# Decode attention with a 16384-long cache: PV with V as the moving operand, and TensorE's order written by hand

## The chip, the core and the metric

The kernel runs on one NeuronCore of a Trainium2 chip. The metric is the device time of one execution in microseconds (us), as the median of the runs. A profile of one execution shows every instruction on TensorE (PE; PEld is its weight load), VectorE (DVE), ScalarE (ACT), GpSimd (POOL) and the queue of SyncE (SP), and the DMA transfers.

## What is computed

One token attends with 32 heads over a cache of 16384 keys and values of width 128. The result goes through an output projection and is mixed, by a scalar gate, with a small gated MLP of the same token. All inputs are bfloat16.

```python
q = (x @ wq).reshape(B, Sq, H, Dh)                # 1 token, H = 32, Dh = 128
scores = einsum('bhqd,bhkd->bhqk', q, k_cache) * Dh ** -0.5
p = softmax(scores)                               # over 16384 keys
o = einsum('bhqk,bhkd->bhqd', p, v_cache)
a = o.reshape(B, Sq, H * Dh) @ wo
g = sigmoid((x * gate_w).sum(-1))
out = g * a + (1 - g) * gmlp(x)                   # gmlp: gelu, layernorm, two projections
```

K and V of one head are 4 MB each, so the caches are 256 MB in all, and each byte is used once.

## The kernel before

**Tiles.** The keys of a head are laid out with 128 consecutive keys per partition: `k_t` and `v_t` are tiles of 128 partitions with 128 slots of 128 values (`(j d)`), 4 MB each. `load_k` (L76) has three buffers, `load_v` (L81) two. Both are issued on SP's queue and wait there, in order, until a buffer is free: K's after the last score matmul that reads it, V's after the last matmul of `attend` that reads it.

**Scores.** There is no transposed K. `qb` holds q on all 128 partitions. `scores_half(h, s)` (L212) works on 64 of the 128 slots: VectorE multiplies K by q in place (L219), TensorE adds up the 128 products in 16 matmuls with the identity as weights (L222, each moves 512 columns, 64 slots of 8 values, into one PSUM tile `s_ps`), and VectorE reduces the remaining 8 values (L224). After the second half ScalarE takes the exponential of the 128x128 scores (L228), which gives `p_t` in bfloat16 and the sums in `L_sb`. `s_ps` has two buffers, so each half has one.

**PV.** `attend(h)` (L232) makes 128 matmuls: each has one slot of V (128 keys by 128 values) as weights and one column of p as the moving operand, and all add into the column h of `o_ps`.

**The loop** (L242): the scores run two heads ahead of PV (`AHEAD`). At head h it loads K of h + 2 and V of h, makes the first half of the scores of h + 2, PV of h, and the second half. After head 1 it calls `gate()` and `mixer()`, which have matmuls on TensorE with small steps of VectorE and ScalarE between them (L144 to L204). V of the last head comes in three pieces. After the loop come the loads of wo, the sum of the softmax denominators (L265), PV of the last head, a rearrangement, and 128 matmuls with wo.

**The order of instructions.** Each engine runs its instructions in the order in the program. That order is not the one in the text: a planner at build time simulates the program with costs of its own and gives each engine the instruction that is ready and stands first in the text. In the kernel before it does this for all engines. Its result for TensorE, from head 2 on, is 29 of a head's 32 score matmuls, then the 128 of PV of two heads before, then the remaining 3. Its result for VectorE is, in one head, first product, second product, first reduction, second reduction; at the start (heads 0 to 2) products of the next head are mixed in. `gate()` comes ahead of all scores, and `mixer()` after those of head 2.

Of the kernel before, what the change touches and what calls it, by code (L numbers as in the profile page):

```python
# [12 lines left out]
FP32 = mybir.dt.float32  # L13
# [4 lines left out]
def kernel(  # L18
# [15 lines left out]
    nc = tc.nc  # L34
# [3 lines left out]
    Dh = 128  # L38
    H = HDh // Dh
# [4 lines left out]
    NJ = Sk // P  # L44
# [7 lines left out]
    const = ctx.enter_context(tc.tile_pool(name="const", bufs=1))  # L52
    kv = ctx.enter_context(tc.tile_pool(name="kv", bufs=2))
    sp = ctx.enter_context(tc.tile_pool(name="sp", bufs=2))
    ps_s = ctx.enter_context(tc.tile_pool(name="ps_s", bufs=2, space=bass.MemoryType.PSUM))
# [18 lines left out]
    vtile = {}  # L74

    def load_k(h):  # L76
        t = kv.tile([P, NJ * Dh], BF16, name="k_t", tag="k", bufs=3)
        nc.sync.dma_start(out=t[:], in_=k_src[h])
        ktile[h] = t

    def load_v(h, cuts=()):  # L81
        t = kv.tile([P, NJ * Dh], BF16, name="v_t", tag="v")
        edges = [0, *cuts, NJ]
        for a, b in zip(edges[:-1], edges[1:]):
            nc.sync.dma_start(out=t[:, a * Dh:b * Dh], in_=v_src[h][:, a * Dh:b * Dh])
        vtile[h] = t
# [3 lines left out]
    ident = const.tile([P, P], BF16, name="ident")  # L90
# [12 lines left out]
                      in_=B_w_in.rearrange("(p c) f -> p (c f)", c=DC))  # L103
    w_out = const.tile([P, FhC, D], BF16, name="w_out")
    nc.sync.dma_start(out=w_out[:].rearrange("p k n -> p (k n)"),
                      in_=B_w_out.rearrange("(p k) n -> p (k n)", k=FhC))
# [3 lines left out]
    for c in range(DC):  # L110
        nc.tensor.matmul(xb_ps[:, c * P:(c + 1) * P], lhsT=x_row[0:1, c::DC], rhs=ones_row[0:1, :],  # L111
                         start=True, stop=True)
# [17 lines left out]
    for i in range(4):  # L130
        nc.vector.tensor_copy(out=sel[:, i, :].rearrange("h (m i) -> h m i", i=4)[:, :, i],
                              in_=ident[0:H, 0:H])

    a_ps = ps_1.tile([P, 512], FP32, name="a_ps")
    o_ps = ps_1.tile([P, H], FP32, name="o_ps")
    g_sb = const.tile([P, 1], FP32, name="g_sb")
# [4 lines left out]
    def gate():  # L141
        gw_ps = ps_m.tile([P, DC + 2], FP32, name="gw_ps", tag="mm")
        for c in range(DC):
            nc.tensor.matmul(gw_ps[:, c:c + 1], lhsT=gw_row[0:1, c::DC], rhs=ones_row[0:1, 0:1],  # L144
                             start=True, stop=True)
        nc.tensor.matmul(gw_ps[:, DC:DC + 2], lhsT=ones_row[0:1, :], rhs=wb_row[0:1, :],  # L146
                         start=True, stop=True)
        gw_col = const.tile([P, DC], BF16, name="gw_col")
        nc.vector.tensor_copy(out=gw_col[:], in_=gw_ps[:, 0:DC])  # L149
        nc.vector.tensor_copy(out=wbf[:], in_=gw_ps[:, DC:DC + 2])  # L150
        g_ps = ps_m.tile([P, 1], FP32, name="g_ps", tag="mm")
        for c in range(DC):
            nc.tensor.matmul(g_ps[:, :], lhsT=xb[:, c, :], rhs=gw_col[:, c:c + 1],
                             start=(c == 0), stop=(c == DC - 1))
        nc.scalar.activation(out=g_sb[:], in_=g_ps[:, :], func=ACT.Sigmoid)
        nc.scalar.activation(out=gm_sb[:], in_=g_ps[:, :], func=ACT.Sigmoid, scale=-1.0)


    def mixer():
        z_ps = ps_m.tile([P, FC], FP32, name="z_ps", tag="mm")  # L160
        w_in5 = w_in[:].rearrange("p c (e m k) -> p c e m k", e=2, k=FhC)
        for fc in range(FC):
            for c in range(DC):
                nc.tensor.matmul(z_ps[:, fc:fc + 1], lhsT=w_in5[:, c, fc // FhC, :, fc % FhC],  # L164
                                 rhs=xb[:, c, 0:1], start=(c == 0), stop=(c == DC - 1))
        z = const.tile([P, FC], FP32, name="z")
        nc.vector.tensor_copy(out=z[:], in_=z_ps[:])
        t = const.tile([P, FC], FP32, name="t")
        nc.vector.tensor_mul(out=t[:], in0=z[:], in1=z[:])
        nc.vector.tensor_scalar(out=t[:], in0=t[:], scalar1=0.044715, scalar2=1.0,  # L170
                                op0=ALU.mult, op1=ALU.add)
        nc.vector.tensor_mul(out=t[:], in0=t[:], in1=z[:])
        nc.scalar.activation(out=t[:], in_=t[:], func=ACT.Sigmoid, scale=1.5957691216057308)
        nc.vector.tensor_mul(out=z[:], in0=z[:], in1=t[:])
        stats = const.tile([P, 2], FP32, name="stats")
        nc.vector.reduce_sum(out=stats[:, 0:1], in_=z[:, FhC:FC], axis=AX.X)
        sq = const.tile([P, FhC], FP32, name="sq")
        nc.vector.tensor_mul(out=sq[:], in0=z[:, FhC:FC], in1=z[:, FhC:FC])
        nc.vector.reduce_sum(out=stats[:, 1:2], in_=sq[:], axis=AX.X)
        tot_ps = ps_m.tile([P, 2], FP32, name="tot_ps", tag="mm")  # L180
        nc.tensor.matmul(tot_ps[:, :], lhsT=ones_f[:, :], rhs=stats[:, :], start=True, stop=True)
        mv = const.tile([P, 2], FP32, name="mv")
        nc.vector.tensor_scalar(out=mv[:], in0=tot_ps[:, :], scalar1=1.0 / Fh, scalar2=0.0,
                                op0=ALU.mult, op1=ALU.add)
        var = const.tile([P, 1], FP32, name="var")
        nc.vector.tensor_mul(out=var[:], in0=mv[:, 0:1], in1=mv[:, 0:1])
        nc.vector.tensor_sub(out=var[:], in0=mv[:, 1:2], in1=var[:])
        rstd = const.tile([P, 1], FP32, name="rstd")
        nc.scalar.activation(out=rstd[:], in_=var[:], func=ACT.Sqrt, bias=eps_t[:, 0:1], scale=1.0)
        nc.vector.reciprocal(out=rstd[:], in_=rstd[:])  # L190
        z2n = const.tile([P, FhC], FP32, name="z2n")
        nc.vector.tensor_scalar(out=z2n[:], in0=z[:, FhC:FC], scalar1=mv[:, 0:1],
                                scalar2=rstd[:, 0:1], op0=ALU.subtract, op1=ALU.mult)
        nc.vector.tensor_scalar(out=z2n[:], in0=z2n[:], scalar1=wbf[:, 0:1],
                                scalar2=wbf[:, 1:2], op0=ALU.mult, op1=ALU.add)
        uf = const.tile([P, FhC], FP32, name="uf")
        nc.vector.tensor_mul(out=uf[:], in0=z[:, 0:FhC], in1=z2n[:])
        u = const.tile([P, FhC], BF16, name="u")
        nc.vector.tensor_scalar(out=u[:], in0=uf[:], scalar1=gm_sb[:, 0:1], scalar2=0.0,  # L199
                                op0=ALU.mult, op1=ALU.add)  # L200
        w_out4 = w_out[:].rearrange("p k (c m) -> p k c m", c=DC)
        for k in range(FhC):
            for c in range(DC):
                nc.tensor.matmul(a_ps[:, c:c + 1], lhsT=w_out4[:, k, c, :], rhs=u[:, k:k + 1],  # L204
                                 start=(k == 0 and c == 0), stop=False, skip_group_check=True)

    L_sb = const.tile([P, H], FP32, name="L_sb")
    p_sb = {}
# [3 lines left out]
    def scores_half(h, s):  # L212
        k3 = ktile[h][:].rearrange("p (j d) -> p j d", d=Dh)
        qh = qb[:, h * Dh:(h + 1) * Dh].unsqueeze(1).broadcast_to([P, NH, Dh])
        if s == 0:
            s_tile[h] = sp.tile([P, NJ], FP32, name="s_sb")
        s_sb = s_tile[h]
        ks = k3[:, s * NH:(s + 1) * NH, :]
        nc.vector.tensor_tensor(out=ks, in0=ks, in1=qh, op=ALU.mult)  # L219
        s_ps = ps_s.tile([P, NH, W], FP32, name="s_ps")  # L220
        for i in range(NS):
            nc.tensor.matmul(s_ps[:, :, :], lhsT=ident[:, :], rhs=ks[:, :, i * W:(i + 1) * W],  # L222
                             start=(i == 0), stop=(i == NS - 1))
        nc.vector.tensor_reduce(out=s_sb[:, s * NH:(s + 1) * NH], in_=s_ps[:, :, :],  # L224
                                axis=AX.X, op=ALU.add)
        if s == 1:
            p_t = sp.tile([P, NJ], BF16, name="p_t", bufs=4)
            nc.scalar.activation(out=p_t[:], in_=s_sb[:], func=ACT.Exp, scale=inv_sqrt_dh,  # L228
                                 accum_out=L_sb[:, h:h + 1])
            p_sb[h] = p_t  # L230

    def attend(h):  # L232
        v3 = vtile[h][:].rearrange("p (j d) -> p j d", d=Dh)
        for j in range(NJ):
            nc.tensor.matmul(o_ps[:, h:h + 1], lhsT=v3[:, j, :], rhs=p_sb[h][:, j:j + 1],  # L235
                             start=(j == 0), stop=(j == NJ - 1))

    AHEAD = 2
    for h in range(AHEAD):
        scores_half(h, 0)  # L240
        scores_half(h, 1)
    for h in range(H - 1):  # L242
        if h > 0:
            if h + AHEAD < H:
                load_k(h + AHEAD)
            load_v(h)
        if h + AHEAD < H:
            scores_half(h + AHEAD, 0)
        attend(h)
        if h + AHEAD < H:  # L250
            scores_half(h + AHEAD, 1)
        if h == 1:
            gate()
            mixer()
    load_v(H - 1, cuts=(64, 96))


    wo_t = kv.tile([P, H * D], BF16, name="wo_t", tag="k", bufs=3)
# [65 lines left out]
```

The softmax here doesn't subtract the row's maximum and nothing guards it: scores larger than these inputs give would overflow.

## Time and profile before

| | |
|---|---|
| median of 3 runs | 665.37 us (665.19 to 666.33) |
| the profiled execution | 665.35 us, span 663.6 us |
| TensorE busy | 429.9 us (65%) |
| VectorE busy | 331.0 us (50%) |
| ScalarE busy | 25.5 us (4%) |
| moved by DMA | 280.31 MB, mean 422 GB/s |
| mean granted TensorE clock | 0.701 |
| score matmuls, L222 | 1024, 310.5 us busy |
| products, L219 | 64, 280.5 us busy, 4421 ns each |
| PV, L235 | 4096, 108.7 us busy |
| reductions, L224 | 64, 44.2 us busy, 691 ns each |

"Busy" is the time in which an engine had at least one instruction under way. Matmuls are pipelined: one score matmul has a record of 376 ns or more, but they can start closer together than that. The granted clock is that of TensorE as a share of full speed. An idle time is put down to what ended it, so a wait for K on VectorE is one in which the landing of K was the last thing missing. Lines of the timeline give start, duration, engine, source line, operation, tiles, count, and in brackets the idle time before and what ended it.

### The profile page before, as it was taken

The page shows a single profiled execution, that of the slowest core. Times are in us where ns is not written, and L with a number is a line of the kernel's source. Part 1 is how long each engine was busy: PE and PEld are TensorE (multiplying, and loading weights), DVE is VectorE, ACT ScalarE, POOL GpSimd, SP SyncE. Part 2 cuts the span into 40 slices and gives each one's busy share as a digit, 9 for nine tenths or more (in the row PEclk, how much of TensorE's full clock was granted, in tenths as well). Part 3 has the DMA queues.
Part 4 walks back from the last instruction along what each step waited for, and adds up shares of the span by engine and source line. Part 5 has one row for each costly group of instructions (what it writes and reads, how often), then busy time and mean ns, then how long its engine had stood idle before and what let it go on. Part 6 is the DMA issues. An engine that isn't in the chain of part 4 may idle for free.

```text
span 663.6 us, 11270 instructions
## 1 busy us (share of the span) xinstructions
PE 429.9 (65%) x5387; PEld 234.3 (35%) x5387; DVE 331.0 (50%) x163; ACT 25.5 (4%) x81; POOL 0.7 (0%) x6
## 2 busy tenths in 40 slices
PE   2777666578566578755668766566766666776574
PEld 0335233344223334422334432333432333433253
DVE  1593655444565444555444556444556553456600
ACT  0402000000000000000000000000000000000000
POOL 0000000000000000000000000000000000000000
PEclk9897656877656677765677765678765667776665
DMA  9999999999999999999999999999999999999986
GB/s 379 439 424 434 426 432 430 432 429 429 432 434 428 431 428 434 433 427 428 434 424 436 430 426 436 430 426 435 427 432 436 424 433 430 428 435 429 428 326 275
DMA packets 10574, 280.31 MB, mean 422 GB/s; under 512 B 1182, under 2 KB 1184, under 8 KB 1568
## 3 DMA queue, kind: packets, MB, share of 16 engines
q1 hardware_dynamic: 10520, 279.58, 98.3%
q8 instruction: 42, 0.69, 0.4%
q14 instruction: 4, 0.03, 0.0%
q10 hardware_dynamic: 8, 0.00, 0.0%
HBM read 279.58 MB, written 0.00 MB: 421 GB/s over the span
## 4 chain that ended last, share of the span: by engine, by line
DMA 69%; PE 21%; DVE 9%; issue 0%; SPq 0%; ACT 0%; ACTq 0%; DVEq 0%
DMA k_t<-in_A_k_cache_dram 66%; PE s_ps L222 16%; DVE k_t L219 9%; PE o_ps L235 5%; DMA wo_t<-in_A_wo_dram 3%; DVE s_sb L224 0%; PE a_ps L285 0%; PE ltot_ps L265 0%; SPq L261 0%; SPq L69 0%; DVE rl L267 0%; ACT p_t L228 0%; PE rT_ps L290 0%; DVE resT L292 0%; DVE res L288 0%
## 5 line engine op out<-in xcount | busy, mean ns | idle before, releaser
L222 PE MATMUL s_ps<-k_t,ident 128*128 128x512 bf16 x1024 | 310.5, 470 | 202.7 <-DVE k_t L219 202.7
L219 DVE TENSOR_TENSOR k_t<-k_t,qb 128x8192 bf16<-128x8192 bf16 x64 | 280.5, 4421 | 43.6 <-DMA k_t<-in_A_k_cache_dram 43.6
L222 PEld LDWEIGHTS <-ident 128*128 128x128 bf16 x1024 | 114.6, 114 | 382.9 <-issue 229.2
L224 DVE TENSOR_REDUCE s_sb<-s_ps 128x64 f32<-128x512 f32 x64 | 44.2, 691 | 240.6 <-PE s_ps L222 240.6
L235 PEld LDWEIGHTS <-v_t 128*128 128x128 bf16 x4096 | 108.6, 97 | 12.7 <-DMA v_t<-in_A_v_cache_dram 5.5
L235 PE MATMUL o_ps<-p_t,v_t 128*128 128x1 bf16 x4096 | 108.7, 163 | 5.2 <-DMA v_t<-in_A_v_cache_dram 5.1
L228 ACT ACTIVATE p_t<-s_sb 128x128 bf16<-128x128 f32 x32 | 9.9, 309 | 593.2 <-DVE s_sb L224 593.2
L121 PE MATMUL q_ps<-wq_t,xb 128*128 128x512 bf16 x32 | 8.8, 445 | 10.7 <-DMA wq_t<-in_A_wq_dram 10.7
L121 PEld LDWEIGHTS <-xb 128*128 128x128 bf16 x32 | 3.6, 112 | 15.7 <-issue 12.2
L285 PE MATMUL a_ps<-o_5855,wo_t 128*128 128x1 bf16 x128 | 3.9, 165 | 4.2 <-DMA wo_t<-in_A_wo_dram 4.2
L124 DVE CAST qb<-q_ps 128x512 bf16<-128x512 f32 x1 | 0.7, 692 | 11.5 <-PE q_ps L121 11.5
L272 DVE TENSOR_TENSOR o_sb<-o_ps,rl 128x32 bf16<-128x32 f32 x1 | 0.2, 192 | 12.0 <-PE o_ps L235 12.0
L228 ACT ACTIVATION_READ_ACCUMULATOR p_t<-s_sb 128x1 f32 x32 | 6.0, 187 | 0.0
L285 PEld LDWEIGHTS <-wo_t 128*128 128x128 bf16 x128 | 3.6, 104 | 4.5 <-DMA wo_t<-in_A_wo_dram 4.5
L126 ACT CAST qb<-q_ps 128x512 bf16<-128x512 f32 x7 | 4.1, 586 | 15.3 <-PE q_ps L121 15.3
L288 DVE CAST res<-a_ps 128x4 bf16<-128x4 f32 x1 | 0.2, 162 | 7.9 <-PE a_ps L285 7.9
L149 DVE CAST gw_col<-gw_ps 128x4 bf16<-128x4 f32 x1 | 0.2, 162 | 6.5 <-PE gw_ps L146 6.5
L164 PEld LDWEIGHTS <-w_in 128*128 128x128 bf16 x56 | 3.2, 153 | 0.5 <-issue 0.5
L164 PE MATMUL z_ps<-xb,w_in 128*128 128x1 bf16 x56 | 3.1, 192 | 0.0
L228 ACT ACT_TABLE_LOAD x2 | 2.6, 1283 | 0.0
L204 PE MATMUL a_ps<-u,w_out 128*128 128x1 bf16 x28 | 0.9, 165 | 2.3 <-DVE u L199 2.3
L111 PE MATMUL xb_ps<-ones_row,x_row 1*128 1x128 bf16 x4 | 0.6, 305 | 2.0 <-DMA x_row<-in_A_x_dram 2.0
(60 smaller groups left out, 19.1 us busy)
## 6 DMA issues: line engine op xcount, KB each, us to landing
k_t<-in_A_k_cache_dram SPq DMA_DIRECT2D x32, 4096.0 KB, 41.8
v_t<-in_A_v_cache_dram SPq DMA_DIRECT2D x31, 4096.0 KB, 33.7
wq_t<-in_A_wq_dram SPq DMA_DIRECT2D x1, 4096.0 KB, 12.5
v_t<-in_A_v_cache_dram SPq DMA_DIRECT2D x1, 2048.0 KB, 9.8
v_t<-in_A_v_cache_dram SPq DMA_DIRECT2D x2, 1024.0 KB, 11.9
wo_t<-in_A_wo_dram SPq DMA_DIRECT2D x1, 2048.0 KB, 17.3
w_in<-in_B_w_in_dram SPq DMA_DIRECT2D x1, 1792.0 KB, 44.1
wo_t<-in_A_wo_dram SPq DMA_DIRECT2D x1, 1024.0 KB
```

Source lines behind the costliest of these rows:

```text
L111: nc.tensor.matmul(xb_ps[:, c * P:(c + 1) * P], lhsT=x_row[0:1, c::DC], rhs=ones_row[0:1, :], start=True, stop=True)
L121: nc.tensor.matmul(q_ps[:, :], lhsT=xb[:, c, :], rhs=wq[:, c, nb * QB:(nb + 1) * QB], start=(c == 0), stop=(c == DC - 1))
L124: nc.vector.tensor_copy(out=qb[:, 0:QB], in_=q_ps[:, :])
L126: nc.scalar.copy(out=qb[:, nb * QB:(nb + 1) * QB], in_=q_ps[:, :])
L164: nc.tensor.matmul(z_ps[:, fc:fc + 1], lhsT=w_in5[:, c, fc // FhC, :, fc % FhC], rhs=xb[:, c, 0:1], start=(c == 0), stop=(c == DC - 1))
L204: nc.tensor.matmul(a_ps[:, c:c + 1], lhsT=w_out4[:, k, c, :], rhs=u[:, k:k + 1], start=(k == 0 and c == 0), stop=False, skip_group_check=True)
L219: nc.vector.tensor_tensor(out=ks, in0=ks, in1=qh, op=ALU.mult)
L222: nc.tensor.matmul(s_ps[:, :, :], lhsT=ident[:, :], rhs=ks[:, :, i * W:(i + 1) * W], start=(i == 0), stop=(i == NS - 1))
L224: nc.vector.tensor_reduce(out=s_sb[:, s * NH:(s + 1) * NH], in_=s_ps[:, :, :], axis=AX.X, op=ALU.add)
L228: nc.scalar.activation(out=p_t[:], in_=s_sb[:], func=ACT.Exp, scale=inv_sqrt_dh, accum_out=L_sb[:, h:h + 1])
L235: nc.tensor.matmul(o_ps[:, h:h + 1], lhsT=v3[:, j, :], rhs=p_sb[h][:, j:j + 1], start=(j == 0), stop=(j == NJ - 1))
L285: nc.tensor.matmul(a_ps[:, c:c + 1], lhsT=wo4[:, k, c, :], rhs=o2[:, k:k + 1], start=False, stop=(k == H - 1), skip_group_check=True)
```

## The change

For the heads 0 to 28, `attend_wide` replaces `attend`. It exchanges the operands: four columns of p are the weights (128 keys by 4), and four slots of V, 512 columns, are moved. There are 32 such matmuls, and they add into a tile `d_ps` of 4 partitions by 512 columns. Of its 4x4 blocks of 128 columns only those on the diagonal hold a product of a p column with its own slot of V. ScalarE copies the tile to `d_sb` in SBUF, and `collect` adds the four diagonal blocks into column h of `o_ps`: four float32 matmuls, with a 4x128 block as weights and one column of a 4x4 identity as the moving operand. The heads 29 to 31 keep `attend`. `d_ps` gets two buffers of its own in the pool of `s_ps`.

The loop, with the scores of heads 0 and 1 ahead of it, is put under `tc.manual_schedule` for TensorE: in this stretch TensorE's instructions keep the order of the text. The other engines are still ordered by the planner. `collect(h)` stands after the second half of the scores of h + 2, and `gate()` and `mixer()` stand after `collect(1)`.

```diff
+    ident_f = const.tile([4, 4], FP32, name="ident_f")
+    nc.vector.tensor_copy(out=ident_f[:], in_=ident[0:4, 0:4])
...
+    R = 512 // Dh
+    diag = {}
+
+    def attend_wide(h):
+        d_ps = ps_s.tile([R, R * Dh], FP32, name="d_ps")
+        NG = NJ // R
+        for g in range(NG):
+            nc.tensor.matmul(d_ps[:, :], lhsT=p_sb[h][:, g * R:(g + 1) * R],
+                             rhs=vtile[h][:, g * R * Dh:(g + 1) * R * Dh],
+                             start=(g == 0), stop=(g == NG - 1))
+        d_sb = sp.tile([R, R * Dh], FP32, name="d_sb")
+        nc.scalar.copy(out=d_sb[:], in_=d_ps[:, :])
+        diag[h] = d_sb
+
+    def collect(h):
+        for r in range(R):
+            nc.tensor.matmul(o_ps[:, h:h + 1], lhsT=diag[h][:, r * Dh:(r + 1) * Dh],
+                             rhs=ident_f[:, r:r + 1], start=(r == 0), stop=(r == R - 1))
+
     AHEAD = 2
-    for h in range(AHEAD):
-        scores_half(h, 0)
-        scores_half(h, 1)
-    for h in range(H - 1):
-        if h > 0:
+    WIDE = H - 3
+    with tc.manual_schedule(engines={mybir.EngineType.PE}):
+        for h in range(AHEAD):
+            scores_half(h, 0)
+            scores_half(h, 1)
+        for h in range(H - 1):
+            if h > 0:
+                if h + AHEAD < H:
+                    load_k(h + AHEAD)
+                load_v(h)
             if h + AHEAD < H:
-                load_k(h + AHEAD)
-            load_v(h)
-        if h + AHEAD < H:
-            scores_half(h + AHEAD, 0)
-        attend(h)
-        if h + AHEAD < H:
-            scores_half(h + AHEAD, 1)
-        if h == 1:
-            gate()
-            mixer()
-    load_v(H - 1, cuts=(64, 96))
+                scores_half(h + AHEAD, 0)
+            if h < WIDE:
+                attend_wide(h)
+            else:
+                attend(h)
+            if h + AHEAD < H:
+                scores_half(h + AHEAD, 1)
+            if h < WIDE:
+                collect(h)
+            if h == 1:
+                gate()
+                mixer()
+        load_v(H - 1, cuts=(64, 96))
```

## The prediction

> **What bounds the kernel now.** I read the page's slices first, then the waits, then the timeline of one head. The slices:
>
> ```profile
> PE   2777666578566578755668766566766666776574
> PEclk9897656877656677765677765678765667776665
> DMA  9999999999999999999999999999999999999986
> ```
>
> The DMA row is full until the last two slices, and one head's K and V (2 x 4096 KB) take a nearly constant time: the first K product of head 3 starts at 69.34 us, that of head 31 at 619.64 us, 550.3/28 = 19.65 us a head. TensorE is busy, but at a clock that moves between half and full. The waits say how much room the compute has:
>
> ```profile
> DVE s_sb L224 <- PE s_ps L222: 240.6, 60, 7.0
> PE s_ps L222 <- DVE k_t L219: 202.7, 34, 7.9
> DVE k_t L219 <- DMA k_t<-in_A_k_cache_dram: 43.6, 30, 2.7
> SPq L78 <- PE s_ps L222: 28.6, 29, 4.2
> ```
>
> (columns: total us, times, longest). VectorE waits for K 30 times, 43.6/30 = 1.45 us each. That is all the room there is between K's arrival and the compute. VectorE and TensorE hand the work to each other in turn, as one head of the timeline shows:
>
> ```profile
> 324.91 8.76 DVE L219 TENSOR_TENSOR k_t<-k_t,qb 128x8192 bf16<-128x8192 bf16 x2 [1.36 <-DMA k_t<-in_A_k_cache_dram]
> 329.38 8.86 PE L222 MATMUL s_ps<-k_t,ident 128*128 128x512 bf16 x29 [6.56 <-DVE k_t L219]
> 335.55 0.69 DVE L224 TENSOR_REDUCE s_sb<-s_ps 128x64 f32<-128x512 f32 x1 [1.88 <-PE s_ps L222]
> 338.08 3.36 PE L235 MATMUL o_ps<-p_t,v_t 128*128 128x1 bf16 x128
> 341.30 1.44 PE L222 MATMUL s_ps<-k_t,ident 128*128 128x512 bf16 x3
> 342.78 0.69 DVE L224 TENSOR_REDUCE s_sb<-s_ps 128x64 f32<-128x512 f32 x1 [6.54 <-PE s_ps L222]
> 344.58 8.76 DVE L219 TENSOR_TENSOR k_t<-k_t,qb 128x8192 bf16<-128x8192 bf16 x2 [1.12 <-DMA k_t<-in_A_k_cache_dram]
> ```
>
> VectorE's order in a head is product, product, reduction, reduction, and the second reduction stands ahead of the next head's product. So a ring closes each head: product 4.43, semaphore 0.04, 29 score matmuls, 128 PV matmuls, 3 score matmuls, reduction 0.69, next product. Its length: over the 29 heads from head 3 on the 29 matmuls' records average 8.58 us, 8.42 from first start to PV's start; PV takes 3.22 to the next start; the three average 1.31. So 4.47 + 8.42 + 3.22 + 1.31 + 0.71 = 18.13 us, 1.52 under the 19.65 that DMA needs, which agrees with the 1.45 waited. The chain of waits puts 69% on DMA and shows this ring only at every third head.
>
> [...] each head's scores start 0.43 us apart, then 0.2155 (16 matmuls in 3.61 us, one record of 0.38: 3.23/15). PV's 3.22 us of one-column matmuls is already enough: of the 30 triples after it only 4 take 0.81 us, the others 1.10 to 1.44, with some at the slow pace. [...] the trace has 80 ns for 128x4 (L290) beside 97 for 128x128. [...]
>
> **The change part by part.**
>
> *Wide PV, heads 0 to 28.* Removed: 128 one-column matmuls, 3.22 us. Added: 32 matmuls of 4 weight columns with 512 moving columns. The trace has none with so few weight columns at this width; the nearest row is L222, the same 512 moving columns and full 128 rows, and V is read without a stride. I take its pitch: 32 x 0.2155 = 6.90 us warm, 32 x 0.43 = 13.8 cold. The weight load (80 to 97 ns) lies beside the matmul before it, as L222's does; so no gain or loss from it.
>
> *Hand order.* TensorE now does 16 scores, 32 wide PV, 16 scores, four collecting matmuls. All 64 wide ones lie inside the ring. Warm they take 64 x 0.2155 = 13.79 us. Cold start: the old 29 cost 8.42 - 29 x 0.2155 = 2.17 us over the warm pace, about ten slow matmuls. In the new ring TensorE streams nothing wide between its last score and the next head's first: reduction 0.71 + product 4.47 = 5.2 us, longer than the 3.22 of PV that pulls the clock down today. So I charge 2.17 once a head; between the halves and PV no gap is left, since V has landed (it waits only 8 times at L235 today) and the second product ends at 8.8 us, before the first 16 scores and PV are through. The three slow scores after PV (1.31) are gone, contained in the 64. Adding the last record's 0.16 drain:
>
> ring = 4.47 + 13.79 + 2.17 + 0.16 + 0.71 = 21.30 us, against 19.65 of DMA. It exceeds it by 1.65 a head. Rings from head 3's product to head 31's: 28, all with wide PV. 28 x 1.65 = +46.2 us. DMA can no longer lead: the stall at L219 on K goes away, and VectorE's wait for S takes its place.
>
> *Will the planner leave the reduction ahead of the next product?* The ring stands on this; only TensorE's order is fixed by hand, VectorE's is the planner's. It put PV after 29 scores everywhere, so in its clock V comes 13 matmuls after the second product made the second half possible: a transfer there lasts 2 products + 13 m, m its matmul. After V the new order has 48 m to the reduction, and the next K comes one transfer later. The reduction stays first if 48 m < 8.86 + 13 m, m < 0.253. With m = 0.2155 it does, by 1.3 us; with m = 0.43 it wouldn't. I take the first.
>
> *Copy of d_ps on ScalarE.* Bound: 0.59 (L126, 128x512) above; ScalarE is at 4%, and 16 scores (3.45 us) cover it. Without that cover: 0.6 a head.
>
> *Collecting matmuls.* Four float32 ones. L265 shows one as two records in 0.65 us: at most 2.6 us, at least 8 x 0.025 (PV's pitch) = 0.2. They stand after the last score, beside the 5.2 us in which VectorE has the ring: nothing. Without that cover up to 2.6 a head.
>
> *Gate and mixer held at h == 1.* Today they fill TensorE's holes: 22.07 to 22.97 and 59.83 to 68.52, 9.6 us with their VectorE steps, while K is awaited. By hand they stand after head 3's scores, and head 4's scores wait behind them. 9.6 - 5.2 = 4.4 if VectorE does its small steps first; 13 if they queue behind two products. I take 6, once.
>
> *Queues.* SP's loads are the same in number and order. V's buffer comes free when wide PV ends, K's after the second half. They wait longest in flight today (33.7 us for V, 41.8 for K, against some 9.8 of transfer each), so over 20 us of lead hides that.
>
> *Tail.* From head 31's product to the end 43.96 us today. If compute is late, V of head 30 is already there and the queue is empty: product 4.47, 16 scores 5.6, old PV 3.2, then V31 with 12.5 (wq's 4096 KB, issue to landing), wo 9.2, last steps 4.0: 39.0. Gain 4.9; 3 to 7 taken as bounds.
>
> Sum: 665.35 (the profiled execution: span 663.6 and 1.75 around it; the median of the runs is 665.37) + 46.2 + 6 - 4.9 = 712.7, so 713. Own range: cold start known to about 0.4 us a head (11), mixer 4.4 to 13, tail 3 to 7: 698 to 734.
>
> **The rivals.**
> (a) *The planner lets the next product go first.* Then VectorE takes K as it lands, the reduction follows, and TensorE alone counts: 13.79 + 2.17 + 2.6 = 18.6 us, under 19.65. DMA bounds as now, the mixer's delay is regained at about 1 us a head, and the old PV of head 29 comes 13 scores earlier, which lets V31 be issued up to 2.8 us sooner; DMA ran at 0.84 in that stretch (619.6 to 640), so up to 1.5 us may come back. 664.5 us, 663.5 to 667: not slower. For it: the product of head 1 does stand ahead of head 0's second reduction at the start (33.28 and 37.61 us), where K lay ready. Against: from head 3 on it never does. It decides as soon as the planner's matmul costs over 0.253.
> (b) *Four weight columns don't hold the clock.* [...] For: today's PV loses the clock. Against: it moves one column each, this moves 512.
> (c) *The clock survives the 5.2 us.* Ring 19.1, under DMA: 665 us. Against: the triples above.
>
> **How the numbers follow.** Forecast 0.64, (a) 0.26, (b) 0.06, (c) 0.04. About 0.2% (1.3 us) is what can be told from no change. Forecast and (b) are slower; (a) and (c) are mostly the same, 0.06 of their 0.30 faster, 0.02 slower: faster 0.06, same 0.22, slower 0.72. The range must reach (a): 663.5 to 735; only (b) and edges lie outside. The forecast alone: 698 to 734.
>
> **What would show it.** Right: 512-column PV at a 0.2155 pitch, head to head 21 us, no wait of L219 on K, DMA under 9 tenths and gaps in it, ten slow scores a head, the reduction ahead of the next product. Wrong: a reduction behind the next product (a), slow pitch within PV (b), fast first scores (c). A wait of the collecting matmuls on ScalarE would show that the copy's cover is gone.

## The result and the profile after

The changed kernel takes 701.36 us (median of 4 runs, 700.91 to 701.54) against 665.38 us: a ratio of 1.0537, with a 95% interval of 1.0519 to 1.0555. It is slower, as forecast, by 36 us where 47.6 were forecast. The profiled execution has a span of 699.7 us.

The slices of the changed kernel:

```profile
PE   2766749979877779777779777789777788777794
PEclk9999778999999888999888999888999988999975
DMA  9999999999999999999999999989999989998557
```

TensorE's clock is now near full speed almost everywhere (mean 0.883 in place of 0.701), and yet the kernel is slower: a faster clock is no aim in itself. The DMA row says little of the new bound: DMA is busy all the time from 150 to 350 us, as before, and 95% of it from 350 to 600 us, where it moves 396 GB/s in place of 430. It had a backlog to live on: K's loads took 41.8 us from issue to landing before and take 24.5 now. So the sign "DMA under 9 tenths" that the prediction named hardly came. The chain of work that ended last shows the change:

```profile
PE 67%; DVE 21%; DMA 11%; issue 0%; SPq 0%; ACT 0%; DVEq 0%
```

It was 69% DMA before. The waits:

```profile
DVE s_sb L227 <- PE s_ps L225: 323.9, 58, 10.7
PE s_ps L225 <- DVE k_t L222: 121.9, 30, 9.1
DVE k_t L222 <- DMA k_t<-in_A_k_cache_dram: 12.4, 3, 7.0
PE d_ps L250 <- DMA v_t<-in_A_v_cache_dram: 1.9, 1, 1.9
```

VectorE waits for K three times in place of 30, the last time at 127.8 us; after that the two engines wait for each other. One head of the timeline:

```profile
320.57 8.75 DVE L222 TENSOR_TENSOR k_t<-k_t,qb 128x8192 bf16<-128x8192 bf16 x2
325.03 4.92 PE L225 MATMUL s_ps<-k_t,ident 128*128 128x512 bf16 x16 [4.13 <-DVE k_t L222]
329.88 7.07 PE L250 MATMUL d_ps<-v_t,p_t 128*4 128x512 bf16 x32
336.89 3.63 PE L225 MATMUL s_ps<-k_t,ident 128*128 128x512 bf16 x16
340.44 1.05 PE L259 MATMUL o_ps<-ident_f,d_sb 4*128 4x1 f32 x8
340.55 0.69 DVE L227 TENSOR_REDUCE s_sb<-s_ps 128x64 f32<-128x512 f32 x1 [9.80 <-PE s_ps L225]
341.16 8.75 DVE L222 TENSOR_TENSOR k_t<-k_t,qb 128x8192 bf16<-128x8192 bf16 x2
```

Read it as a ring: product, 16 scores, 32 wide PV, 16 scores, second reduction, and the next head's product at once, without a wait for K. The collecting matmuls (1.05 us) lie beside the reduction and the product; the idle 4.13 us before the next scores is what is left of VectorE's turn. VectorE keeps this order also where the next K is there: that of head 17 landed at 342.78 us, and VectorE still sat idle for 9.80 us ahead of head 16's second reduction at 362.78 and began head 17's product at 363.39. From head 7 on (product at 152.40 us) to head 31 (658.60) every ring has this form: 506.2/24 = 21.09 us a head, where the kernel before took (619.64 - 147.23)/24 = 19.68.

### The profile page after: what moved, and what is told of

Its sections match the earlier page's. It is cut to its first block, busy times and chain, and to the rows that moved or that the text cites. A ratio compares the mean times of both kernels' runs of the same rounds, so it can differ in the third digit from the quotient of the medians.

```text
span 699.7 us, 6196 instructions
## 1 busy us (share of the span) xinstructions
PE 543.7 (78%) x2835; PEld 237.6 (34%) x2835; DVE 328.2 (47%) x164; ACT 39.5 (6%) x108; POOL 0.7 (0%) x6
## 4 chain that ended last, share of the span: by engine, by line
PE 67%; DVE 21%; DMA 11%; issue 0%; SPq 0%; ACT 0%; DVEq 0%
PE s_ps L225 38%; PE d_ps L250 28%; DVE k_t L222 18%; DMA k_t<-in_A_k_cache_dram 8%; DMA wo_t<-in_A_wo_dram 3%; DVE s_sb L227 2%; PE o_ps L239 0%; PE o_ps L259 0%; SPq L85 0%; PE a_ps L316 0%; SPq L292 0%; PE a_ps L207 0%; PE tot_ps L184 0%; SPq L69 0%; ACT rstd L192 0%
## 5 line engine op out<-in xcount | busy, mean ns | idle before, releaser
L225 PE MATMUL s_ps<-k_t,ident 128*128 128x512 bf16 x1024 | 285.2, 442 | 121.9 <-DVE k_t L222 121.9
L222 DVE TENSOR_TENSOR k_t<-k_t,qb 128x8192 bf16<-128x8192 bf16 x64 | 280.4, 4416 | 12.4 <-DMA k_t<-in_A_k_cache_dram 12.4
L250 PE MATMUL d_ps<-v_t,p_t 128*4 128x512 bf16 x928 | 205.0, 379 | 1.9 <-DMA v_t<-in_A_v_cache_dram 1.9
L225 PEld LDWEIGHTS <-ident 128*128 128x128 bf16 x1024 | 110.2, 110 | 282.8 <-issue 202.3
L250 PEld LDWEIGHTS <-p_t 128*4 128x4 bf16 x928 | 76.5, 85 | 128.0 <-issue 14.2
L254 ACT COPY d_sb<-d_ps 4x512 f32<-4x512 f32 x29 | 16.7, 575 | 464.1 <-PE d_ps L250 464.1
L259 PEld LDWEIGHTS o_ps<-ident_f,d_sb 4*128 4x128 f32 x232 | 27.9, 186 | 12.3 <-issue 12.3
L259 PE MATMUL o_ps<-ident_f,d_sb 4*128 4x1 f32 x232 | 30.4, 248 | 0.0
L239 PE MATMUL o_ps<-p_t,v_t 128*128 128x1 bf16 x384 | 10.3, 164 | 1.9 <-issue 1.9
L239 PEld LDWEIGHTS <-v_t 128*128 128x128 bf16 x384 | 10.2, 99 | 2.2 <-issue 1.9
## 6 DMA issues: line engine op xcount, KB each, us to landing
k_t<-in_A_k_cache_dram SPq DMA_DIRECT2D x32, 4096.0 KB, 24.5
```

The costliest lines, as they stand in the source:

```text
L250: nc.tensor.matmul(d_ps[:, :], lhsT=p_sb[h][:, g * R:(g + 1) * R], rhs=vtile[h][:, g * R * Dh:(g + 1) * R * Dh], start=(g == 0), stop=(g = ...
L254: nc.scalar.copy(out=d_sb[:], in_=d_ps[:, :])
L259: nc.tensor.matmul(o_ps[:, h:h + 1], lhsT=diag[h][:, r * Dh:(r + 1) * Dh], rhs=ident_f[:, r:r + 1], start=(r == 0), stop=(r == R - 1))
```

## The experiments

Nine kernels follow, each with its ratio to the kernel before, of runs on the same chip, and the 95% interval of that ratio. A head with the old PV is called narrow. Three theories stand against each other. *Ring*: the 64 wide matmuls of a head, a cold start among them (in the head above the first scores start 0.427 us apart, at a granted clock of 0.50 from 324.30 to 327.72 us, and the later ones 0.216 us apart, at 1.00), lie between a head's product and the next head's, because the second reduction stands ahead of that product on VectorE. *Occupancy*: TensorE simply has too much to do (78% busy). *Order by hand*, or later release of V's buffers, or contention: something beside the ring.

**1. Hand order, old PV everywhere.**

```diff
-    WIDE = H - 3
+    WIDE = 0
```

> Hand order on TensorE kept, PV of all heads the old way (128 one-column matmuls). Ring theory: product 4.4, 16 scores from a cold start 5.4, PV 3.2, 16 scores after PV, cold again for about 10 of them, 5.4, reduction 0.7 = 19.2 us a head, still under the 19.65 of DMA; DMA bounds, the mixer's place costs a few us that are hardly regained: 667 us (664 to 671). Rival, the hand order itself is what costs: 690 or more. Rival, TensorE's occupancy: 665.

Measured: 665.12 us, ratio 0.9998 (0.9989 to 1.0007). The hand order of TensorE costs nothing that can be told; the mixer's delay was regained too. The total came out as expected, its parts didn't: where K lay ready (heads 4 to 6) a narrow ring took 17.0 us in place of 19.2, since the 16 scores after PV ran at the full clock there (3.61 us).

**2. Wide PV, order left to the planner.**

```diff
-    with tc.manual_schedule(engines={mybir.EngineType.PE}):
+    if True:
```

> Wide PV kept, TensorE's order left to the planner (29 scores, 32 wide, 3 scores, mixer in the early hole; on VectorE the second reduction stands ahead of the next product in every head from 2 on). Ring theory: the same 64 matmuls in the ring, 21.1 us a head, in all 28 rings instead of 24, no delay by the mixer: 665 + 28 x 1.44 - 3 = 703 us (698 to 707). Rival, the hand order is to blame: 665 to 670.

Measured: 709.96 us, 1.067 (1.0654 to 1.0686). This is slower than with the hand order, and above the expected range (698 to 707). The 28 rings take (665.74 - 72.19)/28 = 21.20 us, 0.1 more than expected each (about 3 in all); head 3's product starts 2.9 us later (72.19 us in place of 69.30), and the tail is 1.5 longer than expected. So the loss came in with the exchange of operands and not with the order by hand, which even helped.

**3. The next head's product ahead of the second reduction.** VectorE's order by hand as well. `sums` is the matmul part of `scores_half`, `reduce` and `product` are its VectorE parts, i counts half heads, and the load of K moves up in the text with its product.

```diff
+        s_ps = sums(i)
+        if i + 2 < 2 * H and (i + 2) // 2 not in ktile:
+            load_k((i + 2) // 2)
+        reduce(i, s_ps)
+        if i + 2 < 2 * H:
+            product(i + 2)
...
-    with tc.manual_schedule(engines={mybir.EngineType.PE}):
+    with tc.manual_schedule(engines={mybir.EngineType.PE, mybir.EngineType.DVE}):
+        product(0)
+        product(1)
```

> The changed kernel with VectorE's order by hand as well: reduction of a half, product of the same half of the next head, so that the next head's product stands ahead of the second reduction and no head's product waits for the head before. All 64 wide matmuls, the copy and the collecting matmuls stay. Ring theory: TensorE needs 13.8 + 2 + 1 = 17 us a head, DMA 19.65 bounds again: 665 us (663 to 668). Rivals, TensorE's occupancy or the later release of the V buffers or contention on the memories: 695 to 702 as in the changed kernel.

Measured: 660.92 us, 0.9936 (0.992 to 0.9953). All of TensorE's work is still there, and 40 us are gone, 4 more than the change had cost, which puts it under the expected range (663 to 668); kernels 5 and 9 look for these 4 us. Its waits, and one head of its timeline:

```profile
DVE k_t L220 <- DMA k_t<-in_A_k_cache_dram: 247.7, 28, 15.7
PE s_ps L231 <- DVE k_t L220: 76.3, 29, 9.0
DVE s_sb L238 <- PE s_ps L231: 43.2, 26, 8.1
```

```profile
320.66 3.63 PE L231 MATMUL s_ps<-k_t,ident 128*128 128x512 bf16 x16
323.35 4.43 DVE L220 TENSOR_TENSOR k_t<-k_t,qb 128x8192 bf16<-128x8192 bf16 x1 [8.91 <-DMA k_t<-in_A_k_cache_dram]
324.22 1.05 PE L278 MATMUL o_ps<-ident_f,d_sb 4*128 4x1 f32 x8
327.69 0.68 DVE L238 TENSOR_REDUCE s_sb<-s_ps 128x64 f32<-128x512 f32 x1
327.83 5.30 PE L231 MATMUL s_ps<-k_t,ident 128*128 128x512 bf16 x16 [2.56 <-DVE k_t L220]
```

The product at 323.35 starts when K lands, while the scores of the head before still run; their reduction follows at 327.69. VectorE waits 8.9 us for K, TensorE is 81% busy. TensorE's work, the use of the buffers and the traffic are what they were, so occupancy, buffer release and contention fall. The edit also moves the load of K in the text; kernel 6 has it in the same place and is slow.

**4. More matmuls, to hold the clock.** After `collect(h)`:

```diff
+                f_ps = ps_m.tile([P, 512], FP32, name="f_ps", tag="mm")
+                for _ in range(11):
+                    nc.tensor.matmul(f_ps[:, :], lhsT=ident[:, :], rhs=qb[:, 0:512],
+                                     start=True, stop=True)
```

> The changed kernel plus 11 matmuls of 512 columns after the collecting ones of each head 0 to 28, into a scratch PSUM tile that nothing reads; VectorE's order as in the changed kernel from head 8 on. They lie in the 5.1 us in which VectorE has the ring. Ring theory with the cold start as the deciding term: the next scores start at the full clock, 16 take 3.5 us instead of 5.4, the ring falls from 21.1 to 19.1 us, under DMA's 19.65: 665 us (663 to 669), though TensorE does 11 x 29 = 319 more wide matmuls. If the clock doesn't matter: 701. If TensorE's occupancy bounds: 701 + 29 x 2.4 = 770.

Measured: 661.88 us, 0.9949 (0.9934 to 0.9964). One head:

```profile
330.36 0.69 DVE L227 TENSOR_REDUCE s_sb<-s_ps 128x64 f32<-128x512 f32 x1 [9.33 <-PE s_ps L225]
330.97 8.75 DVE L222 TENSOR_TENSOR k_t<-k_t,qb 128x8192 bf16<-128x8192 bf16 x2
331.24 2.55 PE L285 MATMUL f_ps<-qb,ident 128*128 128x512 bf16 x11
335.44 3.61 PE L225 MATMUL s_ps<-k_t,ident 128*128 128x512 bf16 x16 [1.66 <-DVE k_t L222]
350.25 8.75 DVE L222 TENSOR_TENSOR k_t<-k_t,qb 128x8192 bf16<-128x8192 bf16 x2
```

The order on VectorE is that of the changed kernel and the ring is closed, but its 16 first scores take 3.61 us in place of 4.9 to 6.5, and the granted clock is 1.00 from 200 to 640 us (0.89 in the changed kernel). The ring is 350.25 - 330.97 = 19.28 us, just under what K needs, and 319 additional matmuls make the kernel 40 us faster (a little under the expected 663 to 669). TensorE is 86% busy, the most of all. So two conditions had to meet for the loss: the ring and the cold start. Taking away either one ends it.

**5. The product first, with the old PV.** Kernel 3 with `WIDE = 0`.

> The kernel with the next head's product ahead of the second reduction, but with the old PV (128 one-column matmuls) in all heads. It asks where the 4 us under the kernel before come from. If from the order (V of head 31 asked for sooner, more room on VectorE): 661 us. If from the wide PV itself (half the instructions on TensorE, so less instruction fetch among the transfers, 0.36 in place of 0.69 MB): 664 to 665. I hold the second for more likely, since the hand order with the old PV gave 665.1.

Measured: 665.18 us, 0.9994 (0.9986 to 1.0003). Without the ring the wide PV is worth 4.3 us (3.9 by the two ratios, as kernels 3 and 5 ran on different chips), and the order alone nothing.

**6. The reduction first, in every head.** Kernel 3 with the product moved in front of its own scores from head 3 on:

```diff
         i = 2 * h + s
+        if h > AHEAD:
+            product(i)
         s_ps = sums(i)
...
-        if i + 2 < 2 * H:
+        if i + 2 < 2 * AHEAD + 2:
             product(i + 2)
```

> The changed kernel with VectorE's order by hand, but the dependent way round in every head from 3 on: product, reduction, product, reduction of one head, then the next head. The start (heads 0 to 2) is as before, the mixer's VectorE steps stand between head 3 and head 4. This is the case that the prediction priced: 28 rings and the mixer in the ring. Ring theory: 665.1 + 28 x 1.44 + 9 for the mixer - 3 in the tail = 712 us (708 to 717). If the order of the two on VectorE has no part in it: 661 as with the product first, or 701 as in the changed kernel.

Measured: 713.39 us, 1.0727 (1.071 to 1.0743). It comes out at the prediction's 713, in part by luck: its runs spread from 711.5 to 714.9, and two errors of the sum pull against each other. From head 4 to head 31 the rings are (670.02 - 98.84)/27 = 21.15 us, 1.50 over DMA's time in place of the 1.65 charged; head 3 to head 4 takes 98.84 - 69.20 = 29.6, so the mixer in the ring costs 8.5 in place of 6. Kernels 3 and 6 differ in nothing but the place of the product on VectorE, and 52 us lie between them.

**7. Wide PV in the second half only.** Kernel 6 with

```diff
-            if h < WIDE:
+            if 15 <= h < WIDE:
```

at both places.

> As the run with the reduction first in every head, but only the heads 15 to 28 have the wide PV, the heads 0 to 14 the old one. Ring theory: 14 wide rings at 21.1 us, the narrow ones at about 19.2 and so held by DMA at 19.5; the mixer's 9 us are partly regained before head 15: 665 + 14 x 1.44 + 4 - 3 = 686 us (682 to 692). If a wide head costs something that isn't a ring (contention, a one-time loss), the narrow heads would be slow as well or the sum would not be half.

Measured: 706.04 us, 1.0608 (1.0592 to 1.0625). The expectation missed by 20 us. A narrow head:

```profile
204.87 4.42 DVE L220 TENSOR_TENSOR k_t<-k_t,qb 128x8192 bf16<-128x8192 bf16 x1
209.34 5.10 PE L231 MATMUL s_ps<-k_t,ident 128*128 128x512 bf16 x16 [5.11 <-DVE k_t L220]
214.28 3.35 PE L260 MATMUL o_ps<-p_t,v_t 128*128 128x1 bf16 x128
214.55 0.69 DVE L238 TENSOR_REDUCE s_sb<-s_ps 128x64 f32<-128x512 f32 x1 [5.26 <-PE s_ps L231]
215.16 4.42 DVE L220 TENSOR_TENSOR k_t<-k_t,qb 128x8192 bf16<-128x8192 bf16 x1
219.63 5.08 PE L231 MATMUL s_ps<-k_t,ident 128*128 128x512 bf16 x16 [2.00 <-DVE k_t L220]
224.75 0.69 DVE L238 TENSOR_REDUCE s_sb<-s_ps 128x64 f32<-128x512 f32 x1 [5.17 <-PE s_ps L231]
225.36 4.42 DVE L220 TENSOR_TENSOR k_t<-k_t,qb 128x8192 bf16<-128x8192 bf16 x1
```

The second product now stands behind the first reduction. With the wide PV (7 us) that is covered; the old one (3.35 us) is too short to cover 0.7 + 4.4, so both products and both cold starts lie in the ring: 225.36 - 204.87 = 20.49 us, again over DMA. The edit had made a second ring. The same sum gives its length, but the run says nothing on the half.

**8. The same with the changed kernel's order:** both products of a head, then both reductions.

```diff
+    held = []
...
-        if h > AHEAD:
-            product(i)
+        if h > AHEAD and s == 0:
+            product(i)
+            product(i + 1)
...
+        if h <= AHEAD or s == 1:
+            if s == 1 and h > AHEAD:
+                reduce(i - 1, held.pop())
+            reduce(i, s_ps)
+        else:
+            held.append(s_ps)
```

> The half-wide kernel once more, with VectorE's order as the changed kernel has it in its late heads: both products of a head, then both reductions, then the next head. PV of the heads 15 to 28 is wide, of 0 to 14 old; the mixer's VectorE steps stand between head 3 and head 4. Ring theory: narrow rings 4.4 + 5.4 + 3.2 + 5.1 + 0.7 = 18.8 to 19.3 us, under DMA, so most of the mixer's 9 us is regained; then 14 wide rings at 21.1: 665 + 2 + 14 x 1.5 - 3 = 685 us (681 to 691). If the loss isn't the ring's, near 701 or near 665.

Measured: 681.78 us, 1.0253 (1.0239 to 1.0267), at the lower end of what was expected. Where the narrow part ends and the wide one begins:

```profile
325.07 8.76 DVE L221 TENSOR_TENSOR k_t<-k_t,qb 128x8192 bf16<-128x8192 bf16 x2 [2.33 <-DMA k_t<-in_A_k_cache_dram]
344.49 8.76 DVE L221 TENSOR_TENSOR k_t<-k_t,qb 128x8192 bf16<-128x8192 bf16 x2 [1.76 <-DMA k_t<-in_A_k_cache_dram]
366.49 8.75 DVE L221 TENSOR_TENSOR k_t<-k_t,qb 128x8192 bf16<-128x8192 bf16 x2
387.73 8.75 DVE L221 TENSOR_TENSOR k_t<-k_t,qb 128x8192 bf16<-128x8192 bf16 x2
```

The narrow part keeps DMA's pace: the product of head 17 starts at 344.49 us, as in the kernel before (344.58), and VectorE waits for K ahead of it. From there the heads are (640.87 - 344.49)/14 = 21.17 us apart and no wait for K is left. Each wide head adds to the loss, and the narrow heads had made up for the mixer.

**9. Where the 4 us come from.** Kernel 3 with small matmuls after `collect(h)`:

```diff
+                f_ps = ps_m.tile([P, 512], FP32, name="f_ps", tag="mm")
+                for _ in range(84):
+                    nc.tensor.matmul(f_ps[:, 0:1], lhsT=ident[:, :], rhs=qb[:, 0:1],
+                                     start=True, stop=True)
```

> The fastest kernel so far (next product ahead of the second reduction, wide PV, 660.9 us) plus 84 matmuls of one column after the collecting ones of each head 0 to 28, into a scratch tile that nothing reads. They take about 84 x 0.027 = 2.3 us a head on TensorE, whose 17 us then come to 19.3, still under DMA's 19.5, and bring the number of TensorE's instructions back to about that of the kernel before. If it is the fewer instructions, and with them fewer instruction fetches among the transfers (0.36 MB in place of 0.69), that make the wide PV 4 us faster where it isn't in a ring: 664 to 666 us. If it is the way in which V is read: 661.

Measured: 663.94 us, 0.998 (0.9973 to 0.9986): 3.0 of the 4.3 us are gone again. The row of the instruction fetches in the list of DMA queues (transfers, MB, share), of kernel 3 first and of this kernel second:

```profile
q8 instruction: 22, 0.36, 0.2%
```

```profile
q8 instruction: 41, 0.67, 0.4%
```

K arrives every (616.47 - 69.29)/28 = 19.54 us in kernel 3, every 19.65 in this one, in kernel 5 and in the kernel before: 3.1 us over the 28 heads. TensorE isn't what is waited for (VectorE waits for K for 235 us in all). So K came later with more TensorE instructions. The starts of the products show in which steps. From head 9 on most heads are 19.3 to 19.7 us apart in these four kernels, and the difference sits in single heads that take 20.6 to 21.0: heads 14, 20 and 27 in the kernel before and in kernel 5, 15, 21 and 28 here, but only 14 and 29 in kernel 3. From the product of one of these to that of the next the fetch queue made eight transfers, of 16 KB and about 1.07 us each, in all four kernels, though that took 293 us in kernel 3 and 118 or 138 in the others. So the delay goes with the fetches, about 1.4 us for eight of them; how a fetch holds up K is not shown. The last 1.3 us lie at the end: from the product of head 31 kernel 5 takes 43.8 us, this one 42.5 and kernel 3 42.4. What causes them stays open.

## Why the prediction was right, and where its sizes were off

The span grew by 699.7 - 663.6 = 36.1 us: 39.0 between the products of head 3 and head 31 (589.3 in place of 550.3), and -2.9 after that. The prediction had 46.2 + 6 - 4.9 = 47.3.

*The bound: 1.5 us of room a head.* Right. Kernel 8 shows it from both sides: with the old PV K is waited for, with the wide one it isn't.

*Wide PV, 6.90 us by L222's pitch.* Right: 7.00 us for 32. The loads of the four-column weights lie beside the matmuls, which start 0.216 us apart. Those loads are hardly shorter than full ones (records of 85 ns, against 97 in the old PV), so the few columns saved nothing. The granted clock is 1.00 through the wide PV of all 29 heads; rival (b), whose time was an estimate, is out. V was waited for once. (The 8 waits at L235 that the prediction counts are four, each seen by the matmul and by its load.)

*The cold start, 2.17 us a head.* Right in kind, a little large: over the 24 rings from head 7 on the first 16 scores average 5.35 us up to PV's start, 1.90 over 3.45. Kernel 4 shows that this term decides: without it the ring is under DMA's time. Rival (c), that the clock survives the gap, was wrong, but its arithmetic (19.1 us) is what kernel 4 measured once the gap was filled (19.28).

*The ring, 21.30 us.* Measured 21.09: the first scores are 0.27 less, the reduction 0.10 less, since the next product starts just before it ends, wide PV and the second half together 0.16 more.

*"28, all with wide PV", and "the reduction stays first".* This is the term that was mis-sized. From head 6 on the planner did keep the reduction first, as the sum in matmul costs had it. For two heads after the mixer, 4 and 5, it did not. Here the first product of head 5 stands ahead of the second reduction of head 4, and that of head 6 ahead of the one of head 5:

```profile
111.65 4.41 DVE L222 TENSOR_TENSOR k_t<-k_t,qb 128x8192 bf16<-128x8192 bf16 x1
121.60 0.69 DVE L227 TENSOR_REDUCE s_sb<-s_ps 128x64 f32<-128x512 f32 x1 [5.54 <-PE s_ps L225]
127.80 4.42 DVE L222 TENSOR_TENSOR k_t<-k_t,qb 128x8192 bf16<-128x8192 bf16 x1 [0.58 <-DMA k_t<-in_A_k_cache_dram]
136.69 0.69 DVE L227 TENSOR_REDUCE s_sb<-s_ps 128x64 f32<-128x512 f32 x1 [4.47 <-PE s_ps L225]
```

So the second reductions of the heads 4, 5 and 6 came 15.1 us apart (the third at 151.79), which paid back most of the mixer's delay. K lay ready at 111.65; that this is why the planner let the product go first fits what the prediction says of head 1 under rival (a), but the planner's own costs are not in the trace. From head 3 to head 7 the changed kernel lost 83.1 - 77.9 = 5.2 us, where I had charged 4 x 1.65 + 6 = 12.6. That is 7.4 of the 11.2 us by which the sum was too large; the 24 later rings make 5.8 (33.8 measured, 39.6 charged), and the tail takes 2.0 back. Kernel 6, which has the reduction first in all heads from 3 on, measured 713.39: the priced case was priced nearly right, but the planner built it in full only for the last 24 of 28 rings.

*The mixer, 6 us.* 8.5 when it stands in the ring (kernel 6), inside the bounds of 4.4 to 13.

*The tail, -4.9.* Measured -2.9: the last head's first 16 scores took 6.55 us, 14 of them at the slow pace of 0.427 us, in place of 5.6 (5.03 in kernel 6, whose tail is -4.4), and from the first issue of V31 (672.85 us) to the last landing of wo (695.7) it took 22.9 us in place of 21.7.

*Copy and collecting matmuls at nothing.* Right: 0.57 us beside the scores, 1.05 us beside VectorE's turn, and no wait for either in the list.

*Rival (a).* Its mechanism is real: kernel 3 is this case for all heads. Its time was 664.5; the 660.9 lie below its range, since it put the smaller number of TensorE instructions at nothing, which by kernel 9 makes 3 of these 4 us.

## What to carry to other kernels

Where two engines hand work to each other once a step, write down the ring (what stands between one step's first instruction and the next step's) and compare it with the transfer time; the room is the wait for the transfer divided by its count, and a longer piece in the ring costs only what goes beyond it. Then look at the order on the other engine: one instruction of the next step moved ahead of the last of this one can open the ring, and it was worth 40 us here without any work removed. An order that a planner makes has to be read head by head: here it was one thing for two heads and another for the rest.

## What the runs showed of the hardware

The cold start is not random in a closed ring. In the changed kernel the first 16 scores take 6.55, 5.69, 5.25, 5.03 and 4.92 us in five heads (11 to 15), and then the same again; kernels 2 and 6 show the same five numbers. Five rings take 341.16 - 235.38 = 105.78 us, and the granted clock repeats with them: in the five heads it is 0.50 for 6.83, 6.83, 3.41, 3.41 and 3.41 us, from 238.97 us on, and again from 344.78 and 450.60 us on, 105.8 us apart. What keeps the clock and the ring in step is not shown. So the cold start of a closed ring isn't the mean that heads paced by K have: in the heads 11 to 30 it was 1.97 us over the full clock, where the kernel before had 2.17. The narrow rings of kernel 7 keep one length too: the products of the heads 10 to 17 start 20.48 us apart.

The full clock could be bought here: with 11 wide matmuls without use, 2.55 us in a gap of 5.1, 1.66 us stayed idle, and the first 16 scores took 3.61 us in every head from 5 on (granted clock 1.00 from 200 to 640 us). The 84 one-column matmuls of kernel 9, 2.25 us in the gap ahead of the first scores, did little: in the heads 11 to 30 15 of 20 first halves still start slow and the mean is 5.00 us, against 17 of 20 and 5.24 in kernel 3. In one head 0.46 us stay idle in place of 2.56, and the 16 scores take 5.30 us in both kernels. Ahead of head 31 they fill the time right up to the first score, which still starts at the slow pace (4.96 us for the 16).

Instructions had a price here, where DMA was busy all the time (share 1.00 from 200 to 500 us in kernels 3 and 5): about 5000 TensorE instructions fewer (matmuls and weight loads) went with 20 fetches fewer and were worth 4 us, though the fetches saved are 0.1% of the bytes.
